# Attention row maxima by relu inside PSUM, reciprocals once a head group, a split copy of the accumulator, and a PSUM bank of its own for h

## The chip, the cores and the metric

The kernel runs on one core of one Trainium2 chip. The metric is the device time of one execution in microseconds. A core has a matrix engine (PE), a vector engine (DVE), a scalar engine (ACT), GpSimd (POOL) and SyncE (SP), which issues DMA transfers. Each works through its own instructions in the order of the program and waits on semaphores for the others. PE writes into PSUM, which has eight banks; a tile of 128 x 512 fp32 numbers fills one bank.

## The reference

A block of 2048 rows and 512 columns: layer norm, attention with 32 heads of 16 columns, a residual, then layer norm and a gated MLP with a product over the sequence, and a second residual.

```python
qkv = (x @ wqkv).reshape(B, S, 3, H, Dh)        # H = 32, Dh = 16, S = 2048
scores = einsum("bhqd,bhkd->bhqk", q, k) * Dh ** -0.5
o = einsum("bhqk,bhkd->bhqd", softmax(scores), v)
h = x + o.reshape(B, S, D) @ wo
z = gelu(layernorm(h) @ w_in); z1, z2 = z[..., :688], layernorm(z[..., 688:])
g = einsum("ts,bsf->btf", w_sp, z2) + b_sp[None, :, None]
out = h + (z1 * g) @ w_out
```

The softmax needs the maximum of each row of 2048 scores ahead of the exponentials.

## The kernel before, in words

**Stages.** First come layer norm and the projections to q, k and v, with the first 11 steps of the row maxima laid between the last projections (`ahead`, `LEAD = 11`). Then the attention loop runs. Then a middle stage makes h and z for 16 blocks of rows (`make_h`, `make_z`), and a last stage multiplies with the spatial weights and writes the output. All engines follow an order written out by hand (`manual_schedule`), so an instruction that waits holds everything behind it on its engine.

**The attention loop.** There are 8 head groups (`hg`) of 4 heads, 4 blocks of 512 queries (`qb`) in each and 16 blocks of 128 keys (`kb`) in each of these. One pass of the loop takes two key blocks; it is called a pair here, and 8 pairs are a query block. The order in a pair is the string

```python
PAIR = "s0 M0 join s2 M4 M1 s1 H s3 invert M2 s5 M3 H out M5 s4 M7 turn s6 s7 M6 P".split()
```

- `s0` to `s7` (`score`, L846 and L855): PE multiplies one head's keys with the queries into one of three PSUM banks, and ACT takes the exponential of it into SBUF.
- `H`, `H` and `P` (`weigh`, L871): PE multiplies exponentials with values and adds to the accumulator `pv`, which has one bank. `P` is the newer key block, the two `H` are the halves of the other one, kept back by one pair.
- `M0` to `M7` (`max_pair`, L223 and L228): the row maxima for queries that come later, 128 queries by 2048 keys and two heads in a pair. PE makes 128 x 512 scores in one of four banks (`bank`, in turn by a count), and DVE reduces them to a maximum. Of the heads with `t = 1` four tiles are reduced one by one (M0, M4, M5, M7). Of the heads with `t = 0` only key quarters 2 and 3 are (M1, M2); quarters 0 and 1 go together through max(a, b) = ((a + b) + |a - b|) / 2: M3 (`minus`) multiplies with k0 - k1 and ACT writes the absolute value to SBUF (L233); M6 (`plus`) multiplies with k0 + k1 and DVE adds the two, halves and reduces in one instruction (L237).
- `out` (`take`, L881): at the start of the next query block DVE copies `pv` to SBUF, and two DMAs send it to `o_scr`. The next `P` opens the accumulator again and so waits for the copy.
- `join` and `turn`: after 8 pairs' maxima DVE finishes them (L242), POOL splits them, DVE transposes them (L259), and DMAs put them beside the queries.
- `invert` (L818): the softmax sums are gathered from `o_scr` by two DMAs two passes before, DVE takes 1/sum of 128 x 16 numbers, and two DMAs write it to `r_scr`; once a query block.

POOL meanwhile scales and splits weights for the later stages.

A row step exists for 256 pairs in all; 11 are done ahead, so 245 pairs of the loop carry M0 to M7 and the last 11 do not. The sums and differences k0 + k1 and k0 - k1 are made in the projection stage (`sums`, L484 to L494) and loaded by `load_uv`.

**The middle stage.** `make_z` and `make_h` take their PSUM tiles from one pool of six banks (`mid_ps`). Before its first `make_z`, the end of the attention stage makes the h of one more block in the bank `ps_l`; DVE evacuates it at L776.

Of the kernel before, what the change touches and what calls it, by code (L numbers as in the profile page):

```python
# [8 lines left out]
F32 = mybir.dt.float32  # L9
# [10 lines left out]
P = 128  # L20
# [39 lines left out]
def block_kernel(ctx: ExitStack, tc: tile.TileContext, x, wqkv, wo, w_in, w_sp4, b_sp, w_out, out):  # L60
# [20 lines left out]

    q_scr = dram.tile([2, H * DH, S], F16, name="q_scr")
    k_scr = dram.tile([2, H * DH, S], F16, name="k_scr")
    uv_scr = dram.tile([2, DB, P // 2, 2, 512], F16, name="uv_scr")
# [60 lines left out]
    uvs = [kpool.tile([KS, 2, 1024], F16, name="uvs0")]  # L145
    qst, mx, turned = {}, {}, {}

    def fixed(t):
# [21 lines left out]
    def load_uv(hg, pieces=range(3)):  # L170
        r = slice(32 * (hg % 2), 32 * (hg % 2) + 32)
        for j in pieces:
            nc.sync.dma_start(
                uvs[hg % 2][j:KS:3, :, :],
                uv_scr[(0, 0, 1)[j], hg // 2, r].rearrange("(p r) i s -> r p (i s)", r=DH))

    def load_v(hg):
        raw = vpool.tile([P, NB, 4 * DH], F32, name="raw")
# [26 lines left out]
    def max_pair(m):  # L205

        g, i = divmod(m, 8)
        hg, qb = divmod(g, NQ)
        q, k, w = qst[g], kst[hg % 2], uvs[hg % 2]
        if i == 0:
            mx[g] = sm.tile([P, 16, 4], F32, name="mx")
            nc.gpsimd.memset(mx[g][:, :8, 3:], LOW)
        c, p = slice(i % 4 * P, i % 4 * P + P), i // 4
        at = lambda t, e: mx[g][:, t * 8 + i, e:e + 1]

        def scores(t, keys, b):  # L220
            r = slice(RG * t, RG * t + KS)
            acc = bank(b)
            nc.tensor.matmul(acc, q[r, p, c], keys[r, p], start=True, stop=True)  # L223
            return acc

        def one(t, e, b):
            acc = scores(t, k[:, :, 512 * e:512 * e + 512], b)
            nc.vector.reduce_max(at(t, e if t else e - 1), acc, axis=AX.X)  # L228

        def minus(b):  # L230
            acc = scores(0, w[:, :, 512:], b)
            ab[0] = sm.tile([P, 512], F32, name="ab")
            nc.scalar.activation(ab[0], acc, AF.Abs)  # L233

        def plus(b):
            acc = scores(0, w[:, :, :512], b)
            nc.vector.tensor_tensor_reduce(ab[0], acc, ab[0], 0.5, LOW, ALU.add, ALU.max, at(0, 0))  # L237

        def finish():
            if i == 7:  # L240
                nm = sm.tile([P, 2, 8], F32, name="nm")
                nc.vector.tensor_reduce(nm.rearrange("p t i -> p (t i)"), mx.pop(g), axis=AX.X,  # L242
                                        op=ALU.max, negate=True)
# [3 lines left out]
                nc.gpsimd.tensor_sub(parts[:, :, 1], nm, parts[:, :, 0])  # L247
                turned[0] = (g, parts)

        ab = {}  # L250
# [18 lines left out]
    with ExitStack() as pre:  # L269
# [188 lines left out]
        def proj_qk(b, n, which, between=lambda d: None):  # L458

            c = slice(n * 512, (n + 1) * 512)  # L460
            acc = next_acc()
            for d in range(DB):
                mm3(acc, wqk[b][0][:, which, d, :], wqk[b][1][:, which, d, :],
                    xT[0][:, d, c], xT[1][:, d, c], d == 0, d == DB - 1)
                between(d)

            def take(by_act=True):
                part = p2.tile([P, 2, 512], F16, name="part", bufs=PB)
                if by_act:
                    nc.scalar.activation(part[:, 0, :], acc, AF.Copy, scale=QK_DOWN)  # L470
                else:
                    nc.vector.tensor_scalar(part[:, 0, :], acc, QK_DOWN, None, op0=ALU.mult)
                nc.vector.scalar_tensor_tensor(part[:, 1, :], acc, QK_DOWN, part[:, 0, :],
                                               op0=ALU.mult, op1=ALU.subtract)
                scr = (q_scr, k_scr)[which]
                nc.sync.dma_start(scr[:, b * P:(b + 1) * P, c].rearrange("i p s -> p i s"), part)
                if which == 1 and n < 2:
                    rest.append(sums)

            def sums():  # L480
                hh = P // 2
                if which == 1 and n < 2:
                    kf[n] = p2.tile([P, 512], F32, name=f"kf{n}", bufs=1)
                    nc.scalar.activation(kf[n][:hh], acc[:hh], AF.Copy, scale=QK_DOWN)  # L484
                    nc.scalar.activation(kf[n][hh:], acc[:hh], AF.Copy, scale=-QK_DOWN if n else QK_DOWN)
                if which == 1 and n == 1:
                    uv = p2.tile([P, 512], F32, name="uv", tag="row", bufs=10)
                    nc.gpsimd.tensor_add(uv, kf[0], kf[1])
                    part = p2.tile([P, 2, 512], F16, name="part", bufs=PB)
                    nc.gpsimd.tensor_copy(part[:, 0, :], uv)  # L490
                    nc.gpsimd.tensor_sub(part[:, 1, :], uv, part[:, 0, :])
                    for i in range(2):
                        nc.sync.dma_start(uv_scr[:, b, :, i, :].rearrange("i p s -> p i s"),
                                          part[hh * i:hh * i + hh])  # L494

            return take

# [316 lines left out]
    def invert():  # L814

        hg, cols, sums, pool = sums_.pop(0)
        rc = pool.tile([P, 16], F32, name="rcp")
        nc.vector.reciprocal(rc, sums)  # L818
        to = four_heads(r_scr.rearrange("(d h) s -> d h s", h=8), hg)[:, :, cols]
        for t in range(2):  # L820
            nc.sync.dma_start(to[t].rearrange("p (r c) -> p r c", c=16), rc[64 * t:64 * t + 64])

    def four_heads(t, hg):

# [4 lines left out]
    with ExitStack() as at:  # L829
        kpool1 = at.enter_context(tc.tile_pool(name="kpool1", bufs=1))  # L830
        kst.append(kpool1.tile([RG + KM, 2, S], F16, name="kst1"))
        uvs.append(kpool1.tile([KS, 2, 1024], F16, name="uvs1"))
# [45 lines left out]
        def take(hg, qb, pool=sm):  # L878

            o = pool.tile([P, 512], F32, name="og", bufs=2)  # L880
            nc.vector.tensor_copy(o, pv[0])  # L881
            for t in range(2):
                nc.sync.dma_start(four_heads(o_scr, hg)[t, :, :, qb * 512:qb * 512 + 512],
                                  o[64 * t:64 * t + 64])

        def gather_sums(hg, qb, pool=sm):

            cols = slice(qb * 512, (qb + 1) * 512)
            sums = pool.tile([P, 16], F32, name="sums")
            for t in range(2):  # L890
                nc.sync.dma_start(sums[64 * t:64 * t + 64], four_heads(o_scr, hg)[t, :, DH, cols].rearrange(
                    "p (r c) -> p r c", c=16))
            sums_[0] = (hg, cols, sums, pool)

        wp = at.enter_context(tc.tile_pool(name="wp", bufs=1))
# [190 lines left out]
        for n in range(0, len(units), 2):  # L1086
# [53 lines left out]
            for tok in PAIR if len(later) < 2 else ():  # L1140
# [524 lines left out]
```

## Time and profile before

| | us |
|---|---|
| median of 3 runs (1705.18 to 1706.04) | 1705.86 |
| the profiled execution's own time | 1703.25 |
| its span in the trace | 1701.5 |
| PE busy | 1687.1 |
| DVE busy | 1431.4 |
| ACT busy | 1338.1 |
| POOL busy | 821.8 |

Busy time is the time in which an instruction was in flight on an engine; instructions on one engine overlap, so how long one takes is not how far apart two of them start. The granted clock of PE is full throughout. The attention loop fills the span from about 190 to 1290 us.

### The profile page before, as it was taken

To read this page: it belongs to the slowest core of one execution; us is meant where nothing else is said; L and a number is where in the kernel's file an instruction comes from. 1 tells how busy PE (TensorE), PEld (TensorE's weight loads), DVE (VectorE), ACT (ScalarE), POOL (GpSimd) and SP (SyncE) were. 2 spreads that over 40 slices of the span, in tenths; PEclk is the share of its full clock that TensorE was granted. 3 is DMA by queue.
4 is the path that set the end of the run, shared out by engine and by line. 5 is a ranking of instruction groups with operands and counts; after the bars stand their busy time and mean duration, and the time that the engine had idled before them with its cause. 6 is when DMAs were issued, how large, how long until landed. Compare 5 with 4: busy or idle time off the path is not lost.

```text
span 1701.5 us, 36391 instructions
## 1 busy us (share of the span) xinstructions
PE 1687.1 (99%) x13410; PEld 634.3 (37%) x13410; DVE 1431.4 (84%) x3011; ACT 1338.1 (79%) x2648; POOL 821.8 (48%) x1070
## 2 busy tenths in 40 slices
PE   9999999999999999999999999999999999999999
PEld 4433222222222222222222222222224666666665
DVE  7588999999999999999999999999955776543444
ACT  4335999999999999999999999999996677211111
POOL 1522867776673266687767777400001778200100
PEclk9999999999999999999999999999999999999999
DMA  5744332343221244344443544300116775664551
GB/s 186 205 113 143 99 89 80 91 94 85 79 66 26 57 119 118 92 147 133 123 124 105 147 143 127 87 14 13 40 34 150 203 198 144 235 229 157 202 215 44
DMA packets 214138, 202.29 MB, mean 119 GB/s; under 512 B 92328, under 2 KB 164840, under 8 KB 213960
## 3 DMA queue, kind: packets, MB, share of 16 engines
q1 hardware_dynamic: 211656, 194.33, 39.9%
q10 hardware_dynamic: 2304, 5.64, 1.1%
q8 instruction: 105, 1.72, 0.4%
q14 instruction: 73, 0.60, 0.1%
HBM read 122.10 MB, written 65.93 MB: 111 GB/s over the span
## 4 chain that ended last, share of the span: by engine, by line
PE 85%; DVE 8%; POOL 2%; DMA 2%; ACT 1%; issue 1%; SPq 1%; POOLq 0%; ACTq 0%
PE pv L871 26%; PE s L846 18%; PE m L223 10%; DVE mx L228 6%; PE acc L107 5%; PE acc L109 5%; PE acc L108 5%; PE g L107 4%; PE g L108 4%; PE g L109 4%; PE acc L772 2%; DVE og L881 1%; DVE ab L237 1%; ACT pt L855 1%; DMA raw<-in_w_sp 0%
## 5 line engine op out<-in xcount | busy, mean ns | idle before, releaser
L855 ACT ACTIVATE pt<-s 128x512 f32<-128x512 f32 x1968 | 1007.1, 638 | 2.7 <-PE m L223 1.5
L228 DVE TENSOR_REDUCE mx<-m 128x1 f32<-128x512 f32 x1510 | 947.0, 682 | 11.8 <-PE m L223 3.0
L846 PE MATMUL s<-qst,kst 50*128 50x512 f16 x2048 | 604.2, 379 | 0.1
L871 PE MATMUL pv<-pt,vst 128*32 128x256 f32 (+1 forms) x6056 | 598.2, 466 | 4.1 <-DVE og L881 1.2
L223 PE MATMUL m<-kst,qst 48*128 48x512 f16 x1510 | 452.4, 381 | 0.1
L846 PEld LDWEIGHTS <-kst 50*128 50x128 f16 x2048 | 131.8, 94 | 352.0 <-issue 323.6
L871 PEld LDWEIGHTS pv<-pt,vst 128*32 128x32 f32 x6056 | 119.5, 108 | 290.0 <-issue 276.6
L223 PEld LDWEIGHTS <-qst 48*128 48x128 f16 x2048 | 159.4, 93 | 174.5 <-issue 124.0
L223 PE MATMUL m<-uvs,qst 48*128 48x512 f16 x504 | 190.7, 380 | 0.4 <-DVE mx L228 0.4
L245 POOL TENSOR_SCALAR nm<-nm 128x16 f32<-128x16 f32 x32 | 6.5, 204 | 361.2 <-DVE nm L242 361.2
L237 DVE CUSTOM_DVE_ANT_0 ab<-m,ab 128x512 f32<-128x512 f32 x252 | 170.3, 676 | 2.7 <-ACT ab L233 2.7
L233 ACT ACTIVATE ab<-m 128x512 f32<-128x512 f32 x252 | 157.8, 626 | 15.8 <-PE m L223 15.1
L1429 ACT ACTIVATE pr<-pr,up 128x304 f32<-128x304 f32 (+1 forms) x32 | 17.0, 574 | 108.7 <-DVE up L1383 108.7
L1032 POOL TENSOR_TENSOR op<-raw,op 128x512 f16<-128x512 f32 x80 | 92.8, 1160 | 6.1
L955 POOL TENSOR_TENSOR raw<-raw 128x512 f32<-128x512 f32 (+1 forms) x84 | 83.1, 989 | 6.7
L960 POOL TENSOR_TENSOR acc_sp<-acc_sp,raw 128x512 f32<-128x512 f32 x63 | 80.3, 1275 | 4.5
L107 PE MATMUL acc<-wi,hT 128*128 128x344 f16 x256 | 79.1, 309 | 3.0 <-DVE xr L776 3.0
L109 PE MATMUL acc<-wi,hT 128*128 128x344 f16 x256 | 79.1, 309 | 0.0
L108 PE MATMUL acc<-wi,hT 128*128 128x344 f16 x256 | 79.1, 309 | 0.0
L1571 POOL TENSOR_TENSOR pr<-pr,z 128x344 f32<-128x344 f32 x8 | 7.3, 910 | 148.4 <-DMA whole<-squares 108.3
L952 POOL TENSOR_SCALAR raw<-raw 128x512 f32<-128x512 f32 (+1 forms) x88 | 52.1, 592 | 19.8 <-DMA raw<-in_wqkv 12.5
L1570 DVE TENSOR_TENSOR pr<-g,v 128x344 f32<-128x344 f32 x8 | 4.1, 516 | 66.3 <-PE g L109 63.5
(253 smaller groups left out, 2280.5 us busy)
## 6 DMA issues: line engine op xcount, KB each, us to landing
raw<-in_w_sp SPq DMA_DIRECT2D x128, 256.0 KB
s_scr<-op SPq DMA_DIRECT2D x64, 256.0 KB
op<-s_scr SPq DMA_DIRECT2D x32, 512.0 KB
a_scr<-op SPq DMA_DIRECT2D x48, 256.0 KB
op<-a_scr SPq DMA_DIRECT2D x24, 512.0 KB
o_scr<-og SPq DMA_DIRECT2D x64, 128.0 KB
qst<-q_scr SPq DMA_DIRECT2D x192, 32.0 KB
kst<-k_scr SPq DMA_DIRECT2D x48, 128.0 KB
```

Of the source, the lines that this page charges most:

```text
L107: nc.tensor.matmul(ps, lh, rh, start=first, stop=False, **kw)
L108: nc.tensor.matmul(ps, lh, rl, start=False, stop=False, **kw)
L109: nc.tensor.matmul(ps, ll, rh, start=False, stop=last, **kw)
L223: nc.tensor.matmul(acc, q[r, p, c], keys[r, p], start=True, stop=True)
L228: nc.vector.reduce_max(at(t, e if t else e - 1), acc, axis=AX.X)
L233: nc.scalar.activation(ab[0], acc, AF.Abs)
L237: nc.vector.tensor_tensor_reduce(ab[0], acc, ab[0], 0.5, LOW, ALU.add, ALU.max, at(0, 0))
L846: nc.tensor.matmul(s, kst[hg % 2][r, p, kb * P:(kb + 1) * P], qst[hg * NQ + qb][r, p, :], start=True, stop=True)
L855: nc.scalar.activation(pts[p, kb][:, t, :], s, AF.Exp, scale=scales_[hg // 2])
L871: nc.tensor.matmul(pv[0][32 * j:32 * j + 32, a:b], vst[hg % 2][:, c:c + 32], pts[j % 2, kb][:, j // 2, a:b], start=kb == 0, stop=kb == NB - 1,
L955: pool.tensor_mul(got[0] if n else acc, got[0], got[0])
L1032: chores.append((lambda: pool.tensor_sub(t[0][:, 1], of(), t[0][:, 0]), TT))
```

## The change

Seven edits:

1. M3 (`over`) multiplies with k0 - k1 as before, and ACT applies relu to the result **in place, in the PSUM bank**. M6 (`onto`) multiplies with k1 and **accumulates onto the same bank** (`start=False`), which then holds relu(a - b) + b = max(a, b), and DVE reduces it like the others. `onto` takes no bank of its own, but the count of banks still goes up by one for it.
2. k0 + k1 is no longer made, stored or loaded; only the difference is.
3. In `ahead`, `over` stands before step 2 instead of after step 5.
4. `take`: DVE copies columns 0 to 255 of `pv`, ACT columns 256 to 511.
5. `gather_sums` and `invert` run once a head group (128 x 64 numbers), but in the last head group still once a query block.
6. `invert` runs when there are sums to invert, by the same token.
7. In the middle stage h has a pool of one bank and z a pool of five.

```diff
-        def minus(b):
-            acc = scores(0, w[:, :, 512:], b)
-            ab[0] = sm.tile([P, 512], F32, name="ab")
-            nc.scalar.activation(ab[0], acc, AF.Abs)
-
-        def plus(b):
-            acc = scores(0, w[:, :, :512], b)
-            nc.vector.tensor_tensor_reduce(ab[0], acc, ab[0], 0.5, LOW, ALU.add, ALU.max, at(0, 0))
+        def over(b):
+            both[0] = scores(0, w, b)
+            nc.scalar.activation(both[0], both[0], AF.Relu)
+
+        def onto(b):
+            r = slice(0, KS)
+            nc.tensor.matmul(both[0], q[r, p, c], k[r, p, 512:1024], start=False, stop=True,
+                             skip_group_check=True)
+            nc.vector.reduce_max(at(0, 0), both[0], axis=AX.X)
...
-        return [four[0], two[0], two[1], minus, four[1], four[2], plus, four[3], finish]
+        return [four[0], two[0], two[1], over, four[1], four[2], onto, four[3], finish]
...
-                    todo.extend(steps[i] for i in (0, 1, 4, 2, 5, 3, 6, 7))
+                    todo.extend(steps[i] for i in (0, 1, 4, 3, 2, 5, 6, 7))
...
-                    nc.scalar.activation(kf[n][:hh], acc[:hh], AF.Copy, scale=QK_DOWN)
-                    nc.scalar.activation(kf[n][hh:], acc[:hh], AF.Copy, scale=-QK_DOWN if n else QK_DOWN)
+                    nc.scalar.activation(kf[n], acc[:hh], AF.Copy, scale=QK_DOWN)
...
-        rc = pool.tile([P, 16], F32, name="rcp")
+        n = sums.shape[1]
+        rc = pool.tile([P, n], F32, name=f"rcp{n}")
...
-            nc.vector.tensor_copy(o, pv[0])
+            nc.vector.tensor_copy(o[:, :256], pv[0][:, :256])
+            nc.scalar.copy(o[:, 256:], pv[0][:, 256:])
...
-            cols = slice(qb * 512, (qb + 1) * 512)
-            sums = pool.tile([P, 16], F32, name="sums")
+            if hg < HG - 1 and qb < NQ - 1:
+                return
+            cols, n = (slice(0, S), S // 32) if hg < HG - 1 else (slice(qb * 512, (qb + 1) * 512), 16)
+            sums = pool.tile([P, n], F32, name=f"sums{n}")
...
-                elif tok == "invert" and kb == 6 and n > NB:
+                elif tok == "invert" and kb == 6 and sums_:
...
-        ps = mid.enter_context(tc.tile_pool(name="mid_ps", bufs=6, space=PSUM))
+        ps = mid.enter_context(tc.tile_pool(name="mid_ps", bufs=5, space=PSUM))
+        ps_h = mid.enter_context(tc.tile_pool(name="mid_h", bufs=1, space=PSUM))
...
-                    for _ in make_h(new, ps.tile([P, 512], F32, name="acc")):
+                    for _ in make_h(new, ps_h.tile([P, 512], F32, name="h")):
```

Below, the built order of each engine's instructions is shown at three places; in brackets stand the semaphores that an instruction waits for. The first is PE at the end of a pair inside the loop: M7, s6, s7, M6, P, then s0 and M0 of the next pair. Before:

```order
L223 MATMUL m_9285<-kst_1822,qst 128x512 [waits DVE_49]
L846 LDWEIGHTS kst_1822
L846 MATMUL s<-qst,kst_1822 128x512 [waits Activation_49]
L846 LDWEIGHTS kst_1822
L846 MATMUL s<-qst,kst_1822 128x512 [waits Activation_49]
L223 LDWEIGHTS qst
L223 MATMUL m_9295<-uvs_1823,qst 128x512 [waits DVE_49]
L871 MATMUL pv<-pt,vst_157 32x512 x4
L846 LDWEIGHTS kst_1822
L846 MATMUL s<-qst,kst_1822 128x512 [waits Activation_49]
L223 LDWEIGHTS qst
L223 MATMUL m_9313<-kst_1822,qst 128x512
```

The same place after the change, where lines of the loop stand one lower:

```order
L223 MATMUL m_9001<-kst_1788,qst 128x512 [waits DVE_49]
L845 LDWEIGHTS kst_1788
L845 MATMUL s<-qst,kst_1788 128x512 [waits Activation_49]
L845 LDWEIGHTS kst_1788
L845 MATMUL s<-qst,kst_1788 128x512 [waits Activation_49]
L236 LDWEIGHTS qst
L236 MATMUL m_8988<-kst_1788,qst 128x512 [waits Activation_49]
L870 MATMUL pv<-pt,vst_157 32x512 x4
L845 LDWEIGHTS kst_1788
L845 MATMUL s<-qst,kst_1788 128x512 [waits Activation_49]
L223 LDWEIGHTS qst
L223 MATMUL m_9028<-kst_1788,qst 128x512 [waits DVE_49]
```

Nothing changed its place. But M6 now writes the bank that M3 opened (`m_8988`) and waits for ACT, where it waited for DVE; and M0 of the next pair, which had nothing to wait for, waits for DVE: by the count it takes the bank that M3 and M6 share.

The second place is ACT around the start of a query block after the change; before, the L881 row is not there.

```order
L854 ACTIVATE pt<-s 128x512 [waits PE_49] x8
L232 ACTIVATE m_2442<-m_2442 128x512 [waits PE_49]
L881 COPY og<-pv 128x256 [waits DVE_49]
L854 ACTIVATE pt<-s 128x512 [waits PE_49] x8
L232 ACTIVATE m_2527<-m_2527 128x512 [waits PE_49]
```

ACT's half of the copy stands behind the relu and waits for DVE's half: the two halves run one after the other.

The third place is PE at the start of the middle stage: the last products of h (in the bank `ps_l`), then the first of z. Before:

```order
L772 LDWEIGHTS o_20575
L772 MATMUL h<-wo_1809,o_20575 128x512
L107 LDWEIGHTS hT [waits DVE_49,DMAHW6_49]
L107 MATMUL acc<-wi_1811,hT 128x344 [waits PE_49]
L108 LDWEIGHTS hT
```

After:

```order
L770 LDWEIGHTS o_19935
L770 MATMUL h<-wo_1775,o_19935 128x512
L107 LDWEIGHTS hT [waits DMAHW6_49]
L107 MATMUL acc<-wi_1777,hT 128x344 [waits Activation_49]
L108 LDWEIGHTS hT
```

The first z no longer waits for DVE; it waits for ACT's half of the last copy of `pv`.

More of the change, by code (lines that the diff above doesn't have):

```diff
@@ L83, in block_kernel @@
     k_scr = dram.tile([2, H * DH, S], F16, name="k_scr")
-    uv_scr = dram.tile([2, DB, P // 2, 2, 512], F16, name="uv_scr")
+    uv_scr = dram.tile([2, DB, P // 2, 512], F16, name="uv_scr")
     v_scr = dram.tile([S, D], F32, name="v_scr")
@@ L144, in block_kernel @@
     kst = [kpool.tile([RG + KM, 2, S], F16, name="kst0")]
-    uvs = [kpool.tile([KS, 2, 1024], F16, name="uvs0")]
+    uvs = [kpool.tile([KS, 2, 512], F16, name="uvs0")]
     qst, mx, turned = {}, {}, {}
@@ L174, in load_uv @@
                 uvs[hg % 2][j:KS:3, :, :],
-                uv_scr[(0, 0, 1)[j], hg // 2, r].rearrange("(p r) i s -> r p (i s)", r=DH))
+                uv_scr[(0, 0, 1)[j], hg // 2, r].rearrange("(p r) s -> r p s", r=DH))
     def load_v(hg):
@@ L248, in finish @@
                 turned[0] = (g, parts)
-        ab = {}
+        both = {}
         four = [lambda b, e=e: one(1, e, b) for e in range(4)]
         two = [lambda b, e=e: one(0, e, b) for e in (2, 3)]
-        return [four[0], two[0], two[1], minus, four[1], four[2], plus, four[3], finish]
+        return [four[0], two[0], two[1], over, four[1], four[2], onto, four[3], finish]
     def max_rows():
@@ L482, in sums @@
                 if which == 1 and n < 2:
-                    kf[n] = p2.tile([P, 512], F32, name=f"kf{n}", bufs=1)
-                    nc.scalar.activation(kf[n][:hh], acc[:hh], AF.Copy, scale=QK_DOWN)
-                    nc.scalar.activation(kf[n][hh:], acc[:hh], AF.Copy, scale=-QK_DOWN if n else QK_DOWN)
+                    kf[n] = p2.tile([hh, 512], F32, name=f"kf{n}", bufs=1)
+                    nc.scalar.activation(kf[n], acc[:hh], AF.Copy, scale=QK_DOWN)
                 if which == 1 and n == 1:
-                    uv = p2.tile([P, 512], F32, name="uv", tag="row", bufs=10)
-                    nc.gpsimd.tensor_add(uv, kf[0], kf[1])
-                    part = p2.tile([P, 2, 512], F16, name="part", bufs=PB)
+                    uv = p2.tile([P, 512], F32, name="uv", tag="row", bufs=10)[:hh]
+                    nc.gpsimd.tensor_sub(uv, kf[0], kf[1])
+                    part = p2.tile([P, 2, 512], F16, name="part", bufs=PB)[:hh]
                     nc.gpsimd.tensor_copy(part[:, 0, :], uv)
                     nc.gpsimd.tensor_sub(part[:, 1, :], uv, part[:, 0, :])
-                    for i in range(2):
-                        nc.sync.dma_start(uv_scr[:, b, :, i, :].rearrange("i p s -> p i s"),
-                                          part[hh * i:hh * i + hh])
+                    nc.sync.dma_start(uv_scr[:, b].rearrange("i p s -> p i s"), part)
             return take
@@ L831, in block_kernel @@
         kst.append(kpool1.tile([RG + KM, 2, S], F16, name="kst1"))
-        uvs.append(kpool1.tile([KS, 2, 1024], F16, name="uvs1"))
+        uvs.append(kpool1.tile([KS, 2, 512], F16, name="uvs1"))
         fixed(kst[1])
```

4 lines of the change are left out of this document (2 added, 2 removed).

## The prediction

> **What bounds the kernel now.** I read the page first: the busy times, then the chain that ended last.
>
> ```profile
> PE 1687.1 (99%) x13410; PEld 634.3 (37%) x13410; DVE 1431.4 (84%) x3011; ACT 1338.1 (79%) x2648; POOL 821.8 (48%) x1070
> ...
> PE 85%; DVE 8%; POOL 2%; DMA 2%; ACT 1%; issue 1%; SPq 1%; POOLq 0%; ACTq 0%
> ...
> L228 DVE TENSOR_REDUCE mx<-m 128x1 f32<-128x512 f32 x1510 | 947.0, 682 | 11.8 <-PE m L223 3.0
> ...
> L237 DVE CUSTOM_DVE_ANT_0 ab<-m,ab 128x512 f32<-128x512 f32 x252 | 170.3, 676 | 2.7 <-ACT ab L233 2.7
> L233 ACT ACTIVATE ab<-m 128x512 f32<-128x512 f32 x252 | 157.8, 626 | 15.8 <-PE m L223 15.1
> ```
>
> The last three rows are the groups that the change touches, with the mean ns of one. By the first two PE bounds everything. Inside the attention loop that is not so sure. Next, the windows: 100 us of the loop (length, then busy us and instructions of PE, PEld, DVE, ACT and POOL, clock, DMA), and one of the middle stage.
>
> ```profile
> 900.00:1000.00 100.00, 99.67 (x906) 28.40 (x906) 99.25 (x193) 99.95 (x204) 72.05 (x90) 1.00 0.47 135
> 1300.00:1400.00 100.00, 100.00 (x628) 61.20 (x626) 71.97 (x245) 66.72 (x138) 63.66 (x71) 1.00 0.79 200
> ```
>
> In the loop three engines look full. ACT runs 204 instructions in 100 us without a gap, one per 0.490 us, and a pair has 9 of them: 4.41 us. In the middle stage only PE is full. The timeline of one pair shows how they hang together.
>
> ```profile
> 668.27 3.61 ACT L855 ACTIVATE pt<-s 128x512 f32<-128x512 f32 x7
> ...
> 668.85 0.39 PE L846 MATMUL s<-qst,kst 50*128 50x512 f16 x1
> 668.85 0.39 PE L223 MATMUL m<-kst,qst 48*128 48x512 f16 x1
> ...
> 669.07 0.38 PE L846 MATMUL s<-qst,kst 50*128 50x512 f16 x1
> ...
> 669.30 1.89 DVE L228 TENSOR_REDUCE mx<-m 128x1 f32<-128x512 f32 x3
> ...
> 670.59 0.38 PE L223 MATMUL m<-uvs,qst 48*128 48x512 f16 x1
> ...
> 671.47 0.39 PE L223 MATMUL m<-kst,qst 48*128 48x512 f16 x1
> ...
> 671.75 0.62 ACT L233 ACTIVATE ab<-m 128x512 f32<-128x512 f32 x1
> ...
> 671.95 0.38 PE L223 MATMUL m<-uvs,qst 48*128 48x512 f16 x1
> ...
> 672.26 1.07 PE L871 MATMUL pv<-pt,vst 128*32 128x512 f32 x8
> ...
> 673.26 0.39 PE L846 MATMUL s<-qst,kst 50*128 50x512 f16 x1
> ```
>
> From s0 (668.85) to the next s0 (673.26) is 4.41 us, exactly ACT's nine instructions. M3 starts at 670.59, but its absolute value (671.75) comes 1.16 us later, since ACT is behind: the exponentials of s0, s2, s1, s3 and s5 are queued ahead of it. It ends at 672.37. M6 has started at 671.95, 0.42 us before, and does not care: only DVE needs both.
>
> **M6 behind the relu.** After the change M6 waits for the relu, which stands where the absolute value stood. How long a wait's release takes is shown by the one wait of PE for DVE's copy of `pv`:
>
> ```profile
> 658.26 0.68 DVE L881 COPY og<-pv 128x512 f32<-128x512 f32 x1
> ...
> 658.99 0.64 PE L871 MATMUL pv<-pt,vst 128*32 128x512 f32 x4
> ```
>
> The copy ends at 658.94, P starts 0.05 later. So in the pair above M6 would start at 672.42 instead of 671.95, 0.47 later. PE waits in order, and behind M6 are P and the next s0. Can ACT catch up, so that the wait dies out? Only as far as s0: its exponential cannot run before s0, and where ACT has been waiting for it:
>
> ```profile
> 659.99 0.39 PE L846 MATMUL s<-qst,kst 50*128 50x512 f16 x1
> ```
>
> ```profile
> 660.41 0.60 ACT L855 ACTIVATE pt<-s 128x512 f32<-128x512 f32 x1
> ```
>
> it ends 1.02 us after s0's start. The loop through both engines is then: 1.02 (s0 to the end of its exponential), 5 x 0.490 = 2.45 (s2, s1, s3, s5, relu), 0.05 (release), 0.31 (M6 to P, 672.26 - 671.95), 1.00 (P to s0, 673.26 - 672.26). That is 4.83 us a pair, 0.42 over today, with nothing hiding it: P and s0 have no other order to stand in, and ACT idles the 0.42 us until s0. The relu's own time is unknown, as no row shows ACT writing to PSUM. I take the 0.62 us of L233, the same shape from the same source. If it is shorter, the vector loop below takes over and little is won; each 0.1 us more costs 24.5 us over 245 pairs, at worst a second pass of 0.490.
>
> The Trainium skill, "TensorE: Matmul & The Clock Gate", Part 2, says that only weight loads are pulled ahead and that matmuls stay in program order. By that, M6's wait holds everything behind it, as in the sum; if later matmuls could pass, the sum would be that of the first rival. The trace agrees: when P waited until 658.99, s0 behind it, of another bank, came only at 659.99, the usual 1.00 later.
>
> **M0 behind M6's reduction.** M6 frees M0's bank only when DVE has reduced it, as DVE's last of seven. The nearest row for the step from matmul to reduction, with DVE idle, is:
>
> ```profile
> 103.74 0.39 PE L223 MATMUL tp<-kst,qst 48*128 48x512 f16 x1
> ```
>
> ```profile
> 104.16 0.69 DVE L228 TENSOR_REDUCE mx<-tp 128x1 f32<-128x512 f32 x1 [0.60 <-PE m L223]
> ```
>
> 0.42 us. Reductions start (1.89 - 0.68)/2 = 0.605 apart (669.30). From M0 to M0: 0.42 + 6 x 0.605 + 0.68 + 0.05 = 4.78 us. That is 0.05 under 4.83, so anything else on DVE comes through. Per query block it also has:
>
> ```profile
> L881 DVE COPY og<-pv 128x512 f32<-128x512 f32 x32 | 21.7, 680 | 10.4 <-PE pv L871 10.4
> L818 DVE RECIPROCAL rcp<-sums 128x16 f32<-128x16 f32 x32 | 7.8, 242 | 0.8 <-DMA sums<-o_scr 0.7
> L242 DVE TENSOR_REDUCE nm<-mx 128x16 f32<-128x64 f32 x32 | 6.7, 209 | 0.1
> L259 DVE STREAM_TRANSPOSE mturned<-mparts 128x32 f16<-128x32 f16 x32 | 6.4, 201 | 0.9 <-POOL mparts L247 0.9
> ```
>
> Half of the copy 0.3, maximum and transpose 0.2 each, the reciprocal now a fourth as often: some 0.7. Slack is 8 x 0.05 = 0.4, so 0.3 is left over. A query block becomes 8 x 4.83 + 0.3 = 38.94. Today's is read from the chain, where the same step returns:
>
> ```profile
> 229.47 2.41 DVE mx L228 x4
> ...
> 264.96 2.41 DVE mx L228 x4
> ```
>
> 35.49 us, 0.21 over 8 x 4.41. The difference is 3.45, times 245/8 = 30.6 blocks: **+105.6 us**.
>
> **The split copy.** It halves DVE's part, which is in the 0.7. ACT's half lies between half of 0.490 us and all of it; I take 0.28. It falls into ACT's new 0.42 us of idle time and ends about 0.33 after the relu's end, where P starts 0.36 after it (0.05 + 0.31): covered, just. Without that cover it is 0.3 x 30.6 = 9 us. The DVE instruction that M6 loses (L237, 676 ns) is replaced by a reduction of the same length (682): nothing.
>
> **1/sum once a head group** takes 21 of 32 reciprocals and their DMAs off DVE and SP; they are counted above. One PE wait for DVE, where a reciprocal waited for its sums (0.4 in the list below), goes: -0.4.
>
> **h's own bank.** The list of PE's waits:
>
> ```profile
> PE acc L107 <- DVE xr L776: 3.0, 1, 3.0
> PE pv L871 <- DVE og L881: 1.2, 6, 0.2
> PE m L223 <- DVE mx L228: 0.4, 1, 0.4
> ```
>
> The first z starts at 1296.09 because one of its pool's banks holds the last h, evacuated late. After the change this z waits for ACT's half of the last copy of `pv`, long done. All of it goes, **-3.0**, if PE stays full behind it as in 1300 to 1400; the bound is 0, should the next DVE chain come late. PE's waits in the loop other than these are tenths of a microsecond.
>
> **The first 11 pairs.** Here ACT has time to spare:
>
> ```profile
> 100.51 0.39 PE L223 MATMUL m<-uvs,qst 48*128 48x512 f16 x1
> ```
>
> ```profile
> 100.96 0.60 ACT L233 ACTIVATE ab<-m 128x512 f32<-128x512 f32 x1 [3.83 <-PE m L223]
> ```
>
> The maxima lie between projections in groups of 4 or 5, so `over` and `onto` are mostly a projection apart, and the relu is done. Twice they collide. Once `onto` follows `over` two steps of 0.22 us later (as 668.85 to 669.07): 0.45 + 0.60 + 0.05 - 0.44 = 0.66 us. Once the next pair's M0 follows `onto` by one step and needs its bank, which DVE reduces as the second of two: 0.42 + 0.605 + 0.68 + 0.05 - 0.22 = 1.54. **+2.2**, between 0 and 3. The copies that go there (k0 + k1) and half of the uv transfers were hidden behind PE's products: nothing.
>
> **Sum.** 105.6 - 0.4 - 3.0 + 2.2 = +104.4. The profiled execution took 1703.25 (1701.5 of span), so 1807.7; the median of the runs is 2.6 over it, so **1810 us**. About 0.2% is what a measurement of this kernel can tell from no change.
>
> **Rivals.**
>
> *The relu is ready when PE comes to M6* (not slower). For that ACT must begin it by 671.28, 0.69 after M3 instead of 1.16: it would have to be a whole instruction further ahead. For it: ACT's work in a pair does not grow, and M3 lies 1.36 us of PE's work ahead of M6 (670.59 to 671.95). Against it: five exponentials of the same pair stand ahead, none of which can precede s0. It would give: -6.4 (0.21 x 30.6, the stall at the copy), -3.0 - 0.4 + 2.2, and +8.6 (0.28 x 30.6, as ACT then is the bound): 1707, no change; with ACT's half hidden 1698. Chance 0.06, half of it faster.
>
> *The bank is the bound, with PE as slow as today.* In the pair above M5 starts at 671.47, 2.62 after M0. If that stretch stays, M0 to M0 is 2.62 + 0.42 + 2 x 0.605 + 0.68 + 0.05 = 4.98, 0.57 over today: 245 x 0.57 = 140, less 1.2 of the other terms, 1845. For it: it needs nothing of ACT. Against it: part of the stretch is s1 waiting for the previous pair's last exponential, and ACT would no longer be behind. Chance 0.15.
>
> *The relu is slower for reading and writing one bank.* With a second pass, 4.83 + 0.49 = 5.32: 245 x 0.91 = 223, about 1928. No row speaks for or against. Chance 0.05.
>
> **How the numbers follow.** The forecast has 0.74. Its lower end is a block without leftovers (8 x 4.83 = 38.64, so 3.15 x 30.6 = 96.4 in place of 105.6; 1801), less 0.03 x 245 = 7 us for rows rounded to 0.01: 1793. Its upper end, with the same 7 us and 9 for an uncovered copy, is 1826. The whole range goes on to the bank rival: 1793 to 1846. Left out are the first and the third rival and the tails. Faster 0.03, same 0.03, slower 0.94.
>
> **What would show it.** In the changed profile: pairs 4.8 to 4.9 us apart; PE waiting about 0.5 us for the relu before M6 in every pair, in the list of waits as PE <- ACT; ACT busy near 91% of the loop instead of 99.9%; M0 starting at or just after s0; no 3.0 us before the first z. If pairs stay at 4.41, the first rival holds; if PE waits for DVE at M0 and the pairs are near 5.0, the second; if the relu's row is over 0.8 us, the third.

## The result and the profile after

The changed kernel takes **1803.05 us** (median of 5 runs, 1802.86 to 1803.95) against 1705.25 us before (5 runs, 1703.53 to 1706.04). The ratio is 1.0578, 95% interval 1.0566 to 1.0590: slower by 98 us, where +104.4 was forecast. The profiled execution took 1803.95 us, with a span of 1802.1 (before 1701.5).

The page after: busy times, the chain that ended last by engine and by line, and the groups that the change touches.

```profile
PE 1763.5 (98%) x13410; PEld 640.3 (36%) x13410; DVE 1427.1 (79%) x2734; ACT 1370.3 (76%) x2672; POOL 821.1 (46%) x1070
...
PE 58%; ACT 38%; issue 2%; POOL 1%; DMA 1%; DVE 0%; SPq 0%; POOLq 0%; DVEq 0%; ACTq 0%
ACT pt L854 31%; PE pv L870 16%; ACT m L232 7%; PE s L845 6%; PE acc L107 5%; PE m L236 5%; PE acc L109 5%; PE acc L108 5%; PE g L107 4%; PE g L108 4%; PE g L109 4%; PE h L770 2%; PE m L223 2%; DMA wg<-in_wqkv 0%; POOL op L1034 0%
...
L232 ACT ACTIVATE m<-m 128x512 f32<-128x512 f32 x251 | 159.3, 635 | 20.1 <-PE m L223 20.1
L238 DVE TENSOR_REDUCE mx<-m 128x1 f32<-128x512 f32 x251 | 170.0, 677 | 0.0
L236 PE MATMUL m<-kst,qst 48*128 48x512 f16 x251 | 93.5, 372 | 29.5 <-ACT m L232 0.5
```

PE still shows 98% busy, so by that row alone little happened. The second row tells: ACT's share of the chain went from 1% to 38%, and its lines are the exponential (L854) and the relu (L232). The relu takes 635 ns in the mean, the absolute value took 626. The same 100 us of the loop as before, as a window:

```profile
900.00:1000.00 100.00, 97.50 (x826) 26.21 (x822) 90.66 (x154) 94.65 (x190) 63.03 (x77) 1.00 0.39 117
```

All three engines that were full have room, and ACT runs 190 instructions where it ran 204: 7% fewer in the same time. A few of the 190 are its new halves of copies, one in a block of 38.8 us, 2.6 here; so a pair of nine takes 9 x 100/187.4 = 4.80 us. The chain of waits through one query block says what the loop consists of (start, length, what):

```profile
202.16 0.50 ACT m L232
...
207.15 0.50 ACT m L232
207.69 0.37 PE m L236
208.06 1.00 PE pv L870 x8
209.06 0.33 PE s L845
209.41 2.56 ACT pt L854 x5
211.97 0.50 ACT m L232
...
240.92 0.50 ACT m L232
```

From relu to relu (207.15 to 211.97) it goes once around: relu, M6, P, s0, five exponentials, relu, 4.82 us. Before, the pieces of this chain were PE's products and, at the copy, DVE's. Ends of matmuls are modelled, so the single pieces of PE are not to be taken to 0.05; the sum is. A query block is 240.92 - 202.16 = 38.76 us, 0.20 over 8 x 4.82; its long pair (202.16 to 207.15) is the one with the copy of `pv`. This is the most frequent block, not the mean: over 30 blocks, P to P, the mean is 38.83 us (before 35.53).

The timeline of a pair without a copy, from the relu on:

```profile
648.68 0.61 ACT L232 ACTIVATE m<-m 128x512 f32<-128x512 f32 x1
...
649.34 0.37 PE L236 MATMUL m<-kst,qst 48*128 48x512 f16 x1
...
649.64 1.07 PE L870 MATMUL pv<-pt,vst 128*32 128x512 f32 x8
650.02 0.68 DVE L238 TENSOR_REDUCE mx<-m 128x1 f32<-128x512 f32 x1
...
650.64 0.39 PE L845 MATMUL s<-qst,kst 50*128 50x512 f16 x1
650.75 0.37 PE L223 MATMUL m<-kst,qst 48*128 48x512 f16 x1
...
651.06 2.56 ACT L854 ACTIVATE pt<-s 128x512 f32<-128x512 f32 x5 [0.29 <-PE s L845]
```

The relu ends at 649.29 and M6 starts 0.05 later. P follows 0.30 behind M6, s0 1.00 behind P, and ACT, idle for 0.29 us, begins s0's exponential 0.42 behind s0. M0 starts 0.11 behind s0 and 0.05 behind the end of M6's reduction (650.70): here M0 waits for the bank, but so little that the pair still takes 4.82. Now a pair with the copy:

```profile
668.08 0.41 DVE L880 COPY og<-pv 128x256 f32<-128x256 f32 x1
...
668.53 0.42 ACT L881 COPY og<-pv 128x256 f32<-128x256 f32 x1
668.71 0.37 PE L236 MATMUL m<-kst,qst 48*128 48x512 f16 x1
...
669.02 1.06 PE L870 MATMUL pv<-pt,vst 128*32 128x512 f32 x8
...
669.61 0.68 DVE L238 TENSOR_REDUCE mx<-m 128x1 f32<-128x512 f32 x1
...
670.01 0.39 PE L845 MATMUL s<-qst,kst 50*128 50x512 f16 x1
...
670.34 0.37 PE L223 MATMUL m<-kst,qst 48*128 48x512 f16 x1
```

ACT's half starts 0.04 behind the end of DVE's half and ends at 668.95, 0.07 before P: covered. But DVE is late by its half, M6's reduction starts 0.90 behind M6 instead of 0.68, ends at 670.29, and M0 stands 0.33 behind s0, with s2 behind M0. Over the whole loop the distance from s0 to M0 goes with the length of the pair: nearly all pairs with up to 0.12 us take 4.82, and with 0.18, 0.25, 0.33 and 0.39 they take 4.84, 4.90 to 4.92, 4.98 to 4.99 and 5.05. After the copy pair shown the distance falls to 0.12, 0.08, 0.03 and 0.00: DVE catches up by 0.03 to 0.05 us a pair.

What the lists of PE's waits say of all this:

```profile
PE m L310 <- ACT junk L297: 1.5, 1, 1.5
...
PE tp L223 <- DVE mx L238: 0.9, 1, 0.9
...
PE m L236 <- ACT m L232: 0.5, 1, 0.5
PE m L223 <- DVE mx L238: 0.3, 1, 0.3
```

The wait for the relu that comes in every pair of the loop does not appear there at all: the one entry of 0.5 is `onto` at 96.81, ahead of the loop, and the 0.3 is one M0 at 801.60. In front of M6 stands s7, whose modelled end reaches over most of the wait; what is left as idle time of L236 is 29.5 us, 0.12 a pair. The 3.0 us of the first z are gone from the list.

By stage, from the first product that writes `pv` (the one that opens the accumulator, ahead of the first P) to the start of the last one: 161.06 (before 158.69) and 1392.74 (before 1289.05). So the time ahead of the loop grew by 2.4 us, the loop by 101.3, and what follows shrank by 3.1; together 100.6, the difference of the spans.

### The profile page after: what moved, and what is told of

The parts are those of the page before. It is cut to its first block, busy times and chain, and to the rows that moved or that the text cites. A ratio compares the mean times of both kernels' runs of the same rounds, so it can differ in the third digit from the quotient of the medians.

```text
span 1802.1 us, 35798 instructions
## 1 busy us (share of the span) xinstructions
PE 1763.5 (98%) x13410; PEld 640.3 (36%) x13410; DVE 1427.1 (79%) x2734; ACT 1370.3 (76%) x2672; POOL 821.1 (46%) x1070
## 4 chain that ended last, share of the span: by engine, by line
PE 58%; ACT 38%; issue 2%; POOL 1%; DMA 1%; DVE 0%; SPq 0%; POOLq 0%; DVEq 0%; ACTq 0%
ACT pt L854 31%; PE pv L870 16%; ACT m L232 7%; PE s L845 6%; PE acc L107 5%; PE m L236 5%; PE acc L109 5%; PE acc L108 5%; PE g L107 4%; PE g L108 4%; PE g L109 4%; PE h L770 2%; PE m L223 2%; DMA wg<-in_wqkv 0%; POOL op L1034 0%
## 5 line engine op out<-in xcount | busy, mean ns | idle before, releaser
L854 ACT ACTIVATE pt<-s 128x512 f32<-128x512 f32 x1968 | 1028.0, 618 | 67.3 <-PE s L845 49.3
L228 DVE TENSOR_REDUCE mx<-m 128x1 f32<-128x512 f32 x1511 | 939.9, 684 | 122.0 <-PE m L223 89.5
L223 PE MATMUL m<-kst,qst 48*128 48x512 f16 x1511 | 426.5, 379 | 0.4 <-DVE mx L238 0.3
L845 PEld LDWEIGHTS <-kst 50*128 50x128 f16 x2048 | 145.6, 93 | 374.3 <-issue 332.0
L223 PEld LDWEIGHTS <-qst 48*128 48x128 f16 x1792 | 130.8, 93 | 131.8 <-issue 109.4
L232 ACT ACTIVATE m<-m 128x512 f32<-128x512 f32 x251 | 159.3, 635 | 20.1 <-PE m L223 20.1
L238 DVE TENSOR_REDUCE mx<-m 128x1 f32<-128x512 f32 x251 | 170.0, 677 | 0.0
L236 PE MATMUL m<-kst,qst 48*128 48x512 f16 x251 | 93.5, 372 | 29.5 <-ACT m L232 0.5
L223 PE MATMUL m<-uvs,qst 48*128 48x512 f16 x251 | 94.8, 378 | 0.0
L939 POOL TENSOR_SCALAR raw<-raw,figs 128x512 f32<-128x512 f32 (+1 forms) x84 | 55.5, 665 | 10.4 <-ACT pt L854 9.1
```

Source lines behind the costliest of these rows:

```text
L232: nc.scalar.activation(both[0], both[0], AF.Relu)
L236: nc.tensor.matmul(both[0], q[r, p, c], k[r, p, 512:1024], start=False, stop=True, skip_group_check=True)
L238: nc.vector.reduce_max(at(0, 0), both[0], axis=AX.X)
L845: nc.tensor.matmul(s, kst[hg % 2][r, p, kb * P:(kb + 1) * P], qst[hg * NQ + qb][r, p, :], start=True, stop=True)
L854: nc.scalar.activation(pts[p, kb][:, t, :], s, AF.Exp, scale=scales_[hg // 2])
```

## The experiments

The prediction's account (theory 1) is that M6's wait for the relu sets the pair. Its rival is the bank: M0 waits for the reduction of M6. Or both would be as late, each enough by itself. The first four runs take these apart and separate the other edits. Each ratio is to the kernel before on the same chip.

**e_ownbank**: the changed kernel, with a bank of its own for M3 and M6; the other maxima share three.

```
-                    steps[i](count[0] % 4)
+                    steps[i]((0, 2, 0, 3, 1, 1, 3, 2)[i])
```

> The changed kernel, but in the loop M3 and M6 have a bank that no other M uses; the other six take three banks in turn. The relu stays where it is, late. Theory 1 (M6's wait for the relu sets the pair): 4.82 us a pair as in the changed kernel, about 1800 us. Theory 2 (M0's wait for the shared bank sets it): 4.41 us, about 1705. Theory 3 (each of the two alone would stretch a pair to about 4.8): 4.82, about 1800.

1796.10 us, ratio 1.0533 (1.0517 to 1.0549). 237 pairs take 4.82 us, P to P, the pairs with a copy too:

```profile
665.60 0.42 ACT L881 COPY og<-pv 128x256 f32<-128x256 f32 x1
...
666.08 1.07 PE L870 MATMUL pv<-pt,vst 128*32 128x512 f32 x8
...
667.08 0.39 PE L845 MATMUL s<-qst,kst 50*128 50x512 f16 x1
667.08 0.39 PE L223 MATMUL m<-kst,qst 48*128 48x512 f16 x1
```

M0 is back beside s0. So the bank is not needed for the 4.82; the wait for the relu makes it alone. The bank costs what else there was: the 4.99 of the copy pair and the like, 7 us in all.

**e_swap**: the changed kernel with M2 and M3 exchanged, so that the relu stands one exponential earlier on ACT. M3 then also takes another bank than the next M0.

```
-"... s3 invert M2 s5 M3 H ..."
+"... s3 invert M3 s5 M2 H ..."
```

> The changed kernel with M3 and M2 in each other's place and nothing else: the relu is one exponential earlier, and by the count of banks M3 and M6 now have a bank that the next M0 doesn't take. All three theories: both waits go, ACT's nine instructions set the pair again, 4.41 us; with 0.28 us per block for ACT's half of the copy, 35.5 to 35.6 us a block, 1702 to 1708 us. If pairs stay above 4.6, in-place relu or accumulation costs something that none of the theories has.

1803.79 us, ratio 1.0578 (1.0562 to 1.0594): nothing won, pairs of 4.85 to 4.86. Theory 1 fell in the form in which it had been put. The timeline shows what came in place of the wait:

```profile
667.82 0.63 ACT L232 ACTIVATE m<-m 128x512 f32<-128x512 f32 x1
...
668.33 0.62 ACT L854 ACTIVATE pt<-s 128x512 f32<-128x512 f32 x1
...
669.01 0.37 PE L845 MATMUL s<-qst,kst 50*128 50x512 f16 x1 [0.48 <-ACT pt L854]
...
669.01 0.39 PE L236 MATMUL m<-kst,qst 48*128 48x512 f16 x1
```

The relu is done at 668.45, in time. But the exponential of s5 has become the sixth, s0's being the first; it ends at 668.95, and s7 waits for its bank: 0.48 us, now in front of M6 instead of at it. What counts, then, is not which instruction PE waits for: six ACT instructions, from s0's exponential on, must be over before PE gets to P. Before the change it was five, since the absolute value was of no concern to PE. This is theory 4 below.

**e_sharedbank**: as e_swap, but with the bank of M3 shared with the next M0 again.

```
-                    steps[i](count[0] % 4)
+                    steps[i]((0, 2, 3, 0, 1, 1, 0, 2)[i])
```

> The changed kernel, but M3 changes places with M2, so that the relu stands one exponential earlier on ACT (its end 2.98 us after s0, M6 due near 3.0), while M3 and M6 still share the bank of the next M0. Theory 1 (relu): 4.41 us a pair, about 1705 us. Theory 2 (bank): M0 to M5 2.44, then 0.42 + 2 x 0.605 + 0.68 + 0.05, 4.80 us a pair and some tenths more per query block, 1798 to 1805. Theory 3 (both): as theory 2.

1808.68 us, ratio 1.0607 (1.0591 to 1.0623); most pairs take 4.855. That is above what any of the three theories gave. It was to show the bank without the relu; since e_swap takes as long without the bank, it can't. Against e_swap the shared bank costs 4.9 us.

**e_undo_relu**: the kernel before with the other edits alone (split copy, 1/sum once a group, h's bank).

```
-            nc.vector.tensor_copy(o, pv[0])
+            nc.vector.tensor_copy(o[:, :256], pv[0][:, :256])
+            nc.scalar.copy(o[:, 256:], pv[0][:, 256:])
...
-                elif tok == "invert" and kb == 6 and n > NB:
+                elif tok == "invert" and kb == 6 and sums_:
...
+        ps_h = mid.enter_context(tc.tile_pool(name="mid_h", bufs=1, space=PSUM))
...
```

> The kernel before with edits 4 to 7 (split copy, 1/sum once a head group, h's own bank), and the absolute value and the fused sum as they were. If ACT bounds the loop before the change: the stall at the copy goes (-6.4) but ACT's half of the copy comes on top (+8.6), h's bank -3.0, sums -0.4: about 1704 us. If PE bounds it: 1695 to 1696. If the other edits, and not the relu, make the change slow: near 1800.

1709.44 us, ratio 1.0024 (1.0015 to 1.0033). Pairs are back at 4.41. So the new way of taking the maxima is the slowdown, and the rest, in this kernel, costs 4 us where I had a gain of 3.4. One wait is the one of 0.4 that the 1/sum edit was to take away (`PE m L223 <- DVE mx L228` in the prediction's list of PE's waits). It is still there, once, and has grown:

```profile
PE m L223 <- DVE mx L228: 1.8, 1, 1.8
```

It stands at the reciprocal of a whole head group, for which DVE waits 1.8 us until the DMA has brought its sums. The two pairs there take 6.61 and 5.71 us, 3.5 more than usual; before, a pair of 5.17 stands in the same place, 0.8 more than usual. The next runs take the parts alone.

**e_take**: before, with the split copy alone (the first three lines of the diff above).

> The kernel before with the split copy of the accumulator alone. By the kernel without the relu, where a block took 35.65 instead of 35.49 us: +0.16 x 30.6 = 5, 1710 us. If the slower part there was the 1/sum once a head group: 1699 to 1705, as the copy's stall gets shorter.

1709.70 us, ratio 1.0029 (1.0019 to 1.0038), +4.2. P's waits for the copy, 1.2 us in 6 places before, are now:

```profile
PE pv L871 <- ACT og L882: 11.1, 29, 0.5
```

Where PE does not wait for the relu, P waits for ACT's half in nearly every block, and the pair with the copy takes 4.84 instead of 4.59 (the block 35.65 instead of 35.49). The halves run one after the other: 0.42 + 0.04 + 0.42 = 0.88 against 0.68 for the whole by DVE. The order of the built program had shown that ACT's half waits for DVE's. The Trainium skill, "PSUM — Partial Sum Buffer", section "PSUM bank collisions raise a hardware error", says that two engines must not touch the same bank and partitions at the same time, two readers included. The waits seen here agree with that rule; no run here tried the halves side by side.

**e_inv**: before, with 1/sum once a head group alone.

```
...
+            if hg < HG - 1 and qb < NQ - 1:
+                return
+            cols, n = (slice(0, S), S // 32) if hg < HG - 1 else (slice(qb * 512, (qb + 1) * 512), 16)
...
```

> The kernel before with 1/sum once a head group alone. Seen in the kernel without the relu: once DVE stood 1.8 us, waiting for the sums of a whole group, and two pairs together took 3.5 us longer; the 21 reciprocals that go are about 0.1 us of DVE's time each where they lie. 1705 to 1708 us. If the reciprocals were on the path: 1700 to 1703.

1705.92 us, ratio 1.0010 (1.0001 to 1.0019), with runs between 1705.13 and 1710.23. That is less than a measurement tells from no change; the forecast -0.4 is not borne out. The trace shows why the wait did not go. It belongs to the sums of the fourth query block of a head group, and that reciprocal is the one that the edit keeps. It now takes 128 x 64 numbers and 543 ns (242 for 128 x 16), and PE's wait there is 1.0 us instead of 0.4. The parts alone (+4.2, +1.1, and -4.2 for h's bank below) add up to +1.1, where e_undo_relu has +4.3; about 2 us of the difference lie in the block with this wait, which takes 39.16 us there, 36.60 and 36.68 with the split copy or the 1/sum alone, and 36.10 before.

**e_hbank**: before, with h's own bank alone.

```
-        ps = mid.enter_context(tc.tile_pool(name="mid_ps", bufs=6, space=PSUM))
+        ps = mid.enter_context(tc.tile_pool(name="mid_ps", bufs=5, space=PSUM))
+        ps_h = mid.enter_context(tc.tile_pool(name="mid_h", bufs=1, space=PSUM))
...
```

> The kernel before with h's own bank in the middle stage alone. The 3.0 us ahead of the first z go and nothing takes their place: 1702 to 1703 us. If the next chain of DVE then comes late: 1705.

1700.53 us, ratio 0.9976 (0.9966 to 0.9986). The first z's 3.0 us are gone from PE's waits, and nothing took their place:

```profile
PE pv L871 <- DVE og L881: 1.3, 6, 0.3
PE acc L538 <- DVE idle L532: 1.2, 1, 1.2
PE acc L107 <- DMA xT<-xp: 0.7, 1, 0.7
```

It gains 4.2 us by the medians, 3.0 was the wait; the interval holds both. This is the best version found. It is ahead of the kernel before by 0.24%: little more than a measurement can tell, but its interval lies below 1.

Now theory 4. If the count of ACT instructions ahead of P makes the pair, then moving M6 away from P must give the time back, with the relu as it is. Against it stands theory 5: the scheme is dear in itself, through the relu in PSUM or the product that adds to it, wherever M6 stands.

**e_pm6**: e_ownbank with P ahead of M6.

```
-"... s6 s7 M6 P"
+"... s6 s7 P M6"
```

> The kernel with a bank of its own for M3 and M6, and M6 after P instead of before it. New theory 4 (a pair is as long as the way from s0 through the ACT instructions that PE's next wait counts on, and back to s0; it was six of them, for M6 here and for s7 with M3 early): s7 now waits for the fifth exponential, 1.02 + 4 x 0.490 + 0.05 = 3.03 us after s0, P 0.31 later, M6 another 1.00, the next s0 0.22 after M6 since both use the same rows of PE: 4.56 us a pair, about 1740 us. Theory 5 (the relu in PSUM or the accumulation onto it is dear in itself): 4.8 or more, 1795 or more.

1765.14 us, ratio 1.0352 (1.0336 to 1.0367). Pairs take 4.60, near the 4.56 of theory 4 and not the 4.8 of theory 5. But the time is 25 us over what I had expected for it, mostly because the copy pairs take 5.29:

```profile
PE pv L870 <- ACT og L881: 19.3, 30, 0.7
```

With P no longer held up by M6, ACT's half of the copy is what P waits for, 0.6 us a block.

**e_defer**: M6 of a pair put into the middle of the next pair, where its relu is long done, with its own bank.

```
-"s0 M0 join s2 M4 M1 s1 H s3 invert M2 s5 M3 H out M5 s4 M7 turn s6 s7 M6 P"
+"s0 M0 s2 M4 M1 s1 H s3 invert M6 join s5 M2 H out M5 s4 M7 s6 s7 M3 turn P"
...
+                elif tok == "M6" and held:
+                    late_ = held.pop()
+                    late_[6](3)
+                    joins.append(late_[8])
...
```

> The changed kernel with M3 in M6's place at the end of a pair, M6 in M2's place of the next pair, M2 in M3's place, and a bank of its own for M3 and M6. The relu is then ACT's ninth instruction, and PE asks for it 1.3 us into the next pair. Theory 4: PE's waits count on five exponentials again, and ACT's nine instructions set the pair: 4.41 us, with the split copy 35.65 us a block as in the kernel without the relu: 1707 to 1713. Theory 5: 4.8 us or more a pair, 1795 or more.

1743.97 us, ratio 1.0226 (1.0211 to 1.0242). Pairs take 4.457: of the 0.41 that the scheme cost, 0.36 is gone though the relu and the adding product are all there. That leaves theory 5 at most the other 0.05, to which e_defer_copy comes back. The total is 31 to 37 us over what I had expected, and again the copy is why. Two pairs a block take 5.33 and 4.75:

```profile
642.09 0.41 DVE L880 COPY og<-pv 128x256 f32<-128x256 f32 x1
...
642.54 0.37 ACT L881 COPY og<-pv 128x256 f32<-128x256 f32 x1 [0.82 <-DVE og L880]
...
642.96 1.07 PE L870 MATMUL pv<-pt,vst 128*32 128x512 f32 x8 [0.80 <-ACT og L881]
```

ACT stands idle for 0.82 us until DVE's half is over, then copies its own, and PE stands for 0.80. The half costs ACT twice: its 0.4 and the wait in its queue, with exponentials behind it.

**e_defer_copy**: e_defer with the whole copy on DVE.

> The kernel with the onto step put off into the next pair, and the accumulator copied by DVE alone again. If the split copy makes that kernel's copy pairs long (5.33 and 4.75 us in place of 4.46, since ACT stands waiting for DVE's half): most of 1.1 us a block goes, 1712 to 1722 us. If it is something else: 1740 to 1745.

1728.44 us, ratio 1.0138 (1.0122 to 1.0153): 15.5 us less than e_defer, still 6 over the expected range. What is left:

```profile
PE pv L870 <- DVE og L880: 20.5, 30, 0.8
```

M6's reduction now stands ahead of the copy in DVE's order, so P waits about 0.7 us a block for it. The other part is the 0.05 a pair that stayed in e_defer. In this stretch, without a copy, ACT works without a gap:

```profile
227.03 0.62 ACT L232 ACTIVATE m<-m 128x512 f32<-128x512 f32 x1
...
227.55 4.07 ACT L854 ACTIVATE pt<-s 128x512 f32<-128x512 f32 x8
```

The next relu starts at 231.49: 0.52 for the relu and 3.94 for eight exponentials, 4.46. Before, it is 0.47 for the absolute value and 3.94 to the next one at 649.49:

```profile
645.08 0.62 ACT L233 ACTIVATE ab<-m 128x512 f32<-128x512 f32 x1
645.55 4.07 ACT L855 ACTIVATE pt<-s 128x512 f32<-128x512 f32 x8
```

Over the loop, where no gap follows, ACT starts its next instruction 0.515 us after the relu here and 0.477 after the absolute value before (medians of 199 and 240). So of the scheme's 0.41 us a pair, some 0.04 are the price of the relu in PSUM, and the rest went with the place of M6.

From P to P a block takes 36.31 us against 35.49 before: 0.38 for eight pairs of 4.457, and 0.44 that the copy costs more than before. 0.82 x 30.6 = 25.1; with the changed kernel's 2.4 ahead of the loop and -3.1 behind it that is 24.4, and 23.7 was measured.

**e_after_copy**: the changed kernel with the whole copy on DVE.

```
-            nc.vector.tensor_copy(o[:, :256], pv[0][:, :256])
-            nc.scalar.copy(o[:, 256:], pv[0][:, 256:])
+            nc.vector.tensor_copy(o, pv[0])
```

> The changed kernel with the accumulator copied by DVE alone. In the changed kernel DVE's chain to the shared bank has 0.05 us of slack a pair: 0.3 us more of copy come through, 0.2 to 0.3 a block, 1809 to 1812 us. If the wait for the relu covers the copy whichever way it is made: 1803.

1810.69 us, ratio 1.0620 (1.0603 to 1.0636), 7.6 us over the changed kernel and as expected. Pairs with a copy take 5.25 instead of 4.99, and PE waits:

```profile
PE m L223 <- DVE mx L238: 6.2, 30, 0.2
```

The same edit that costs 4.2 us in the kernel before saves 7.6 here: DVE's queue decides when M6's bank is free, and the half that ACT takes from DVE shortens it.

**e_direct** is about the kernel before. I had said that ACT sets its loop. In one pair of eight, both quarters are reduced by DVE directly; ACT has one absolute value less in a block, and DVE one reduction more.

```
...
+        if i == 6 and m >= LEAD:
+            minus, plus = lambda b: one(0, 0, b), lambda b: one(0, 1, b)
```

> The kernel before; in one pair of each query block (245 pairs have 31 of these) M3 and M6 multiply with k0 and k1 and DVE reduces both, with no absolute value on ACT. If ACT bounds the loop before the change: ACT loses 0.49 us a block, DVE has 0.6 more and some room: 0.3 to 0.49 a block, 1690 to 1696 us. If PE bounds it: 1704 to 1706. If DVE bounds it: +0.6 a block, 1720 or more.

1715.76 us, ratio 1.0062 (1.0048 to 1.0076), +10:

```profile
900.00:1000.00 100.00, 99.65 (x902) 28.01 (x900) 99.51 (x192) 99.00 (x201) 78.38 (x95) 1.00 0.44 126
```

ACT's freed 0.49 us a block did not become time. DVE has 0.605 more to do and the block grew by 10.3 / 30.6 = 0.34. So DVE was within 0.3 us a block of being the bound itself. That ACT alone sets the loop before was too much said: ACT and DVE are both full.

## Why the prediction was right, and where it was off

**M6 behind the relu: right, and it is nearly the whole slowdown.** By terms: the release took 0.05 (0.05 forecast), M6 to P 0.30 (0.31), P to s0 1.00 (1.00). From s0 to the end of the relu there is left 4.82 - 1.35 = 3.47, as forecast. Two small errors cancel in it: the five steps of ACT take 2.40 us (651.06 to the relu at 653.46) and not 2.45, and the last instruction, the relu, takes 0.65 there and not the 0.60 of an exponential. That nothing hides it is shown by e_defer: with M6 half a pair later, 0.36 of the 0.41 come back.

**M0 behind M6's reduction: right, a little too dear.** It was forecast 0.05 under the relu's loop and is: M0 comes closer to s0 by 0.03 to 0.05 us a pair, and taking the bank away leaves the pair at 4.82. What is left over of DVE's other work was put at 0.3 a block and is 38.83 - 8 x 4.82 = 0.27 in the mean. A block grew by 3.30 us in the mean, where 3.45 was forecast: 0.08 of this is a pair of 4.82 for 4.83, 0.03 the leftovers, and 0.04 that one block of 35.49 stood for all, whose mean is 35.53. Times 30.6 that is some 4.6 us. Against it stand about 0.5 by which the first pair grew as well, and the -0.4 that did not come; so the loop grew by 101.3 and not by 105.2.

**The split copy: covered, for the reason given.** ACT's half takes 0.42, not 0.28, and still ends 0.07 before P. No wait of P for ACT is in the list. The case without cover, 9 us, has its counterpart in e_take: 4.2.

**1/sum: the step failed.** It was to take away a wait of 0.4; alone the edit measures +1.1, within what can't be told from nothing. The wait is that for a group's last sums, which the edit does not move: it is 1.0 in e_inv, 1.8 in e_undo_relu and 0.3 in the changed kernel, where the pair with it takes 5.35. DVE also saves less than was counted: 11 of 32 reciprocals stay, a third and not a fourth, and the seven of a whole group take 545 ns each in the changed kernel instead of 242.

**h's bank: right.** What follows the loop shrank by 3.1 (-3.0).

**The first 11 pairs: both waits right, the sum in part by luck.** The two forecast waits are in the list: M0 of the next pair for the reduction of `onto` (0.9) and `onto` for the relu (0.5). Held against the same projection products before, PE falls back by 1.32 us at the first (92.71) and by 0.64 at the second (96.81), where 1.54 and 0.66 were forecast; together 1.96. The measured +2.4 has two parts more. A lag of 0.9 us is there at the first of these products already, to which the wait of L310 on top of the list, 1.5 against 0.9 before, adds 0.6. That wait comes ahead of all maxima and is between 0.6 and 1.9 in the runs that list it. And 0.4 is won back at about 150 us.

**What was to show it.** The length of the pairs, M0 at or just after s0, and the first z came as said. The list of waits did not show PE <- ACT in every pair, as I had said it would. ACT is 94.65% busy, not 91: it idles 0.29 a pair, since the last instruction before a gap counts with its full 0.6 us instead of 0.49. And the first sentence on the loop, that ACT's nine instructions set it, holds for the number 4.41 but not as the sole cause (e_direct).

The swap of M2 and M3 would have been my advice, had the study ended with the prediction: a wait named correctly, but with the next one right behind it.

## What to carry to other kernels

Where an in-order engine is made to wait for another one's result, count what must have run on that other engine since their last common point, not which instruction is named in the wait: moving the relu one place forward moved the wait to s7 and won nothing, while moving M6 itself a half pair later gave back nearly all of the 0.41 us a pair (the kernel as a whole, with the copy back on DVE, stayed 1.4% over the one before). An edit's sign depends on whose queue is late: the same split of a copy cost 4.2 us in one kernel and saved 7.6 in the other. Measure bundled edits alone; the best version here is one of them, h's own bank.

## What the runs showed of the hardware that was not expected

- A relu from PSUM into the same bank of PSUM takes 635 ns in the mean (128x512), an absolute value from PSUM to SBUF 626 ns; ACT's next instruction starts 0.515 us after the one and 0.477 after the other. Function and destination differ both, so no run here says which of them costs it. The Trainium skill, "ScalarE: Activation LUTs", section "Step-by-step: what each stage is for", says that ScalarE writes PSUM faster than SBUF; these rows show no such gain.
- Half of a copy is not half as long. The groups of the changed kernel, by line, have 416 ns on DVE and 419 on ACT for 128x256, where 128x512 took 680 on DVE:

```profile
L881 ACT COPY og<-pv 128x256 f32<-128x256 f32 x32 | 13.4, 419 | 1.7 <-DVE mv L781 1.7
L880 DVE COPY og<-pv 128x256 f32<-128x256 f32 x32 | 13.3, 416 | 10.8 <-PE pv L870 10.8
```

- A matmul held up for about 0.4 us behind another one leaves PE looking busy: 98%, with such a wait in nearly all of 245 pairs. The chain and the distance from P to P show it, the busy share and the list of waits don't.
